# A second round's fourth and fifth attention pair, run as one burst of twelve score tiles

## The chip, the core and the metric

The kernel runs on one core of a Trainium2 chip. The metric is the device time of one execution in microseconds (us), the median of several runs. TensorE (PE, with its weight loads PEld), VectorE (DVE), ScalarE (ACT), GpSimd (POOL) and SyncE (SP) each work through their own list of instructions in order. All transfers between the chip's DRAM and its on-chip memory are issued from SP's list.

## The reference

For 8 batches, 12 heads, 448 positions and a head size of 64, sigmoid attention feeds a gated layer with a product over positions:

```python
scores = scale * np.matmul(q, k.transpose(0, 1, 3, 2)) - np.log(S)
attn = 1.0 / (1.0 + np.exp(-scores))
x = np.matmul(attn, v)                      # then to (batch, seq, 768)
h = np.maximum(x @ w_in, 0.0)               # 768 -> 1024
u, v = h[..., :512], h[..., 512:]
v_n = (v - mean(v)) / np.sqrt(var(v) + 1e-06)
v_s = np.einsum('ts,bsd->btd', w_spatial, v_n) + b_spatial[None, :, None]
out = (u * v_s) @ w_out                     # 512 -> 768
```

All of it is in 32-bit floats. Where one product on TensorE isn't exact enough, the kernel splits an operand into a high and a low part and adds three products.

## The kernel before, in words

**Rounds.** The work runs in four rounds `m` of two batches each. A round has attention (`first_attention` for the first, `attention(m)` for the others), then `v_half` (values through `w_in`), `spatial`, `u_half` and `outputs`. The attention of a round consists of six *pairs* `p` = 0 to 5; a pair is two units (one unit is two heads of one batch), and has six full score tiles (`FIRST` and `SECOND`) and one short one that holds the last 64 keys.

**A pair's work.** For a score tile, TensorE multiplies six times (three products for each of two heads, line 340) into a PSUM tile `psc`, then ACT takes the sigmoid into a tile `at` (line 350). When the tiles of a pair are there, TensorE multiplies them with the values (line 376) into `pav`, and DVE copies `pav` out (`whole`, line 1171). `pair(p)` (line 1185) does six score tiles and then six products. `double(p, extra, early, between, late)` (line 1222) does two pairs as one burst: twelve score tiles, then twelve products. It needs PSUM room, so three of the tiles (`k` = 2, 4, 6) are copied out by DVE first (`move`, lines 1247 and 1249) and the sigmoid is taken later in place (line 1242). It also needs two places more than the ring `free` of tiles has: `extra` names places for the tiles 4 and 6. The hooks `early`, `between` and `late` hold the loads that are issued inside the burst.

**Which rounds do what.** Rounds `m` = 2 and 3 run pair 0, then `double(1)`, then `double(3)` with `extra`. Round `m` = 1, the second, runs `pair(0)`, `double(1)`, `pair(3)`, `pair(4)`. All rounds then do the short tiles (from line 1369) and `pair(5)`.

**Sums that only the second round makes.** During the attention of round 1, POOL forms sums of weights for later rounds, as two generators (`u_sums`, `v_sums`) of which `load_weights(n)` takes the next `n` steps. `v_sums` (line 635) has twelve stages. A stage writes a high and a low part on POOL (a CAST, line 657, and a TENSOR_TENSOR, line 658) into one of four staging tiles, and each fourth stage first makes four differences (line 655) in the tile `v_vals`. A step of the generator issues the store of stage `n` to `tv_dram` on SP (line 664) and then the work of stage `n + 4` on POOL, which overwrites the staging tile that this store reads, so that POOL waits for the store to land. `v_vals` lives in the first half of a large tile, `whole`, that takes turns (tag `shared`) with the output factors of `factors(m)`; its other half is not used.

**What follows on SP.** After the last step of `v_sums`, SP issues four loads of 768 KB (`block_load`, line 1300) into that same large tile, now `factors`, and the first product of `v_half` (line 395, `pv<-factors,x_s`) needs the first of them. The stores, these loads, the loads of the short tiles (`last_loads`, line 1157) and the loads of values (`value_loads`, line 284) all stand in SP's one list. Buffers of values are three (tag `v`), so the load of pair 5's values waits until the last product of pair 3 is done.

**Splits.** `attention_splits` makes the high and low part of a raw tile of queries and keys, in the second round's later pairs on DVE (lines 116 and 117). `following(p)` with the table `groups` says which pairs' splits a pair or burst makes. `last_of_four` names the units whose split stands in the last chunk of `x_s`.

Of the kernel before, what the change touches and what calls it, by code (L numbers as in the profile page):

```python
# [36 lines left out]
def attn_gmlp_kernel(  # L37
# [25 lines left out]
    nc = tc.nc  # L63
    B, NHP, _, _ = qk.shape
    S = out.shape[3]
    D = P // 2
    NCC = out.shape[1]
    DM = NCC * P
    F = w_in.shape[1] // (4 * NCC)
# [27 lines left out]
    mark = small.tile([1, 1], F32, name="mark", bufs=1)  # L97
# [163 lines left out]
    def load_weights(n):  # L261
        for _ in range(n):
            next(weights[0], None)
# [14 lines left out]
    def value_loads(b, hp):  # L278
        vt = work.tile([P, 2 * NFULL + 1, P], F32, tag="v", name=f"v_{b}_{hp}", bufs=3)
        values[b, hp] = vt  # L280
        if b == hp == 0:
            nc.sync.dma_start(vt[:, :NFULL], v[b, hp // 2, :, :NFULL])
        else:
            nc.sync.dma_start(vt, v[b, hp // 2])
# [828 lines left out]
    def attention(m):  # L1113

        first = 2 * NHP * m
        free = []
        last_of_four = (5,) if m == 1 else (5, 9)
        shorts, wholes, lasts, held = {}, {}, {}, {}
        copy = nc.vector.tensor_copy

        def unit(p):
            return units[first + 2 * p]

        def loads(*ns):
            for n in ns:
                attention_loads(*units[first + n])
# [19 lines left out]
        def last_loads(p):  # L1146
            b, hp = unit(p)
            if p in (0, 1, 3, 4):
                raw = work.tile([P, 1024], F32, tag="raw", name=f"last_{b}_{hp}", bufs=4)
                raw = raw.rearrange("p (u c) -> p u c", u=2)  # L1150
            else:
                raw = slot(free, f"last_{b}_{hp}")
                held[p] = free.pop()
            lasts[p] = raw
            for here, there in ((slice(0, HALF), 0), (slice(HALF, HALF + S), HALF + REST)):
                there = slice(there, there + here.stop - here.start)
                nc.sync.dma_start(raw[:, :, here], qk[b, hp : hp + 2, :, there].rearrange("u p c -> p u c"))
# [52 lines left out]
                low_part(n)  # L1210
            return pav

        groups = [(0,), (1, 2), (3,), (4,)] if m == 1 else [(0,), (1, 2), (3, 4)]

        def following(p):
            ends = [g[-1] for g in groups]
# [5 lines left out]
        def double(p, extra, early, between, late=None):  # L1222

            tiles = [(*unit(r), t) for r in (p, p + 1) for t in (*FIRST, *SECOND)]
            ats, tag_of, scores = {}, {}, {}
# [48 lines left out]
                sigmoid(then)  # L1274
            product_of(5)
            sigmoid(6, ats[6])
            nc.scalar.copy(mark, (ats[6][0][:1, :1] if extra else ats[6][:1, 0, :1]))
            product_of(2)
            copy_sums(p, product_of(4), copy)
            between()  # L1280
# [18 lines left out]
        def block_load(k):  # L1299
            nc.sync.dma_start(v_block(m, k).bitcast(F32), w_v_dram[:, k])  # L1300
# [4 lines left out]
        def last_value_loads():  # L1305
            last_v = work.tile([P, 2 * NFULL + 1, P], F32, tag="v", name=f"last_v_{m}", bufs=3)
            last_vs.append(last_v)
            lasts_of = v[2 * m : 2 * m + 2, :, :, NFULL].rearrange("b g p c -> p b g c")
            for i, b, gs in ((0, 0, slice(0, 2)), (2, 0, slice(2, 3)), (3, 1, slice(0, 3))):
                nc.sync.dma_start(last_v[:, i : i + gs.stop - gs.start], lasts_of[:, b, gs])  # L1310

        def after(p):
            for u in ((0, 3), (1, 4, 2, 5))[p - 3]:
                last_loads(u)
            if p == 3:
                value_loads(*unit(5))
            load_weights((3, 8)[p - 3])
            if p == 4:
                for k in range(4):
                    block_load(k)  # L1320

        def second_inside():
            value_loads(*unit(4))
            load_weights(1)

        def inside(p):
            value_loads(*unit(p + 3 - p // 3))
            if p == 3:
                last_loads(2)
            block_load(p)  # L1330

        def early_lasts():
            last_loads(1)
# [2 lines left out]
        extra = []  # L1336
        if m > 1:
            halves_of = [other_tiles(f"oat_{m}", F32)]
            halves_of.append([work.tile([P, 512], F32, tag="wval", name=f"wat_{m}_{i}", bufs=2) for i in range(2)])
            extra = [[t[:, :S] for t in ts] for ts in halves_of]  # L1340
        if m == 1:
            pair(0)
            loads(6, 7)
            value_loads(*unit(3))
            load_weights(1)
            loads(8, 9)
            load_weights(1)
            double(1, [], lambda: None, second_inside)
            loads(10, 11)
            last_value_loads()  # L1350
            load_weights(2)
            for p in (3, 4):
                pair(p)
                after(p)
        else:
            pair(0)
            loads(6, 7)
            value_loads(*unit(3))
            block_load(0)
            loads(8, 9)  # L1360
            double(1, [], lambda: None, lambda: inside(1))
            loads(10, 11)
            last_value_loads()
            block_load(2)
            for u in (0, 3):
                last_loads(u)
            double(3, extra, early_lasts, lambda: inside(3), lambda: last_loads(5))
        last_v, = last_vs
        first_ones, others_of = (0, 3, 1), (4, 2, 5)
        for p in first_ones:  # L1370
# [213 lines left out]
```

## Time and profile before

| what | value |
|---|---|
| median of 3 runs | 633.63 us (632.96 to 634.17) |
| the profiled execution's own time | 632.0 us |
| its span, first to last instruction | 630.2 us |
| PE busy | 625.9 us, 99% |
| DVE busy | 453.7 us, 72% |
| ACT busy | 344.6 us, 55% |
| POOL busy | 106.1 us, 17% |
| DMA | 116.66 MB, mean 185 GB/s |

All times in the rows are counted from the span's start. The profiled execution is 1.6 us below the median of the runs. A "busy" PE is one that has a matmul in its pipe; the share says how little room there is between its matmuls.

### The profile page before, as it was taken

Reading aid. Unit: us, or ns where it says so; the run is one execution under the profiler, and the core shown is the slowest. Engines: PE = TensorE matmul, PEld = TensorE weight load, DVE = VectorE, ACT = ScalarE, POOL = GpSimd, SP = SyncE. Lnnn points to the kernel's source line nnn. Section 1 sums busy time; section 2 is a strip of 40 time slices with the busy share of each in tenths; the row PEclk is TensorE's granted clock in tenths of the full one; section 3 lists DMA queues with packets and bytes.
Section 4 is the critical chain, followed back from the end, with each engine's and each line's share of the span. In section 5 each row is a group of like instructions: output and inputs, shape, how many; then the busy total and the mean of one; then the engine's idle time right before and its main releaser. Section 6 shows DMA issues by size and latency. Waiting matters only on the chain.

```text
span 630.2 us, 10405 instructions
## 1 busy us (share of the span) xinstructions
PE 625.9 (99%) x4029; PEld 492.7 (78%) x4029; DVE 453.7 (72%) x666; ACT 344.6 (55%) x549; POOL 106.1 (17%) x168
## 2 busy tenths in 40 slices
PE   9999999999999999999999999999999999999997
PEld 5555789999765479999975549999997535999997
DVE  6888779998866697356777589635777649845485
ACT  6889385225476776612346696750317667673040
POOL 0000111064968731100000003110000002110000
PEclk9999999999999999999999999999999999999999
DMA  8877731156888876262286924508038681452204
GB/s 315 288 253 221 245 120 33 35 200 255 298 290 289 260 261 231 106 229 99 82 269 233 303 87 161 201 25 327 30 109 319 226 274 51 163 189 56 96 29 147
DMA packets 47746, 116.66 MB, mean 185 GB/s; under 512 B 9040, under 2 KB 26320, under 8 KB 47440
## 3 DMA queue, kind: packets, MB, share of 16 engines
q1 hardware_dynamic: 47696, 115.98, 53.0%
q8 instruction: 32, 0.52, 0.3%
q14 instruction: 18, 0.15, 0.1%
HBM read 91.59 MB, written 24.38 MB: 184 GB/s over the span
## 4 chain that ended last, share of the span: by engine, by line
PE 99%; DVE 1%; issue 0%
PE pav L376 20%; PE pv L395 17%; PE psc L340 14%; PE pw L395 11%; PE pg L395 11%; PE ux L395 7%; PE uy L395 5%; PE pu L395 5%; PE px L395 4%; PE psc L322 3%; DVE whole L1176 0%; PE idle L1481 0%; PE psc L332 0%; PE last L395 0%; DVE cs L1010 0%
## 5 line engine op out<-in xcount | busy, mean ns | idle before, releaser
L350 ACT ACTIVATE at<-psc,bias_s 128x896 f32<-128x896 f32 x105 | 97.7, 1015 | 71.3 <-PE psc L340 53.0
L376 PE MATMUL pav<-at,v 128*64 128x448 f32 (+1 forms) x596 | 113.1, 542 | 0.0
L376 PEld LDWEIGHTS pav<-at,v 128*64 128x64 f32 (+1 forms) x596 | 39.3, 136 | 63.6 <-issue 50.1
L340 PEld LDWEIGHTS psc<-qks 64*128 64x128 f32 x762 | 69.9, 184 | 17.2 <-issue 10.1
L340 PE MATMUL psc<-qks 64*128 64x448 f32 x762 | 82.0, 365 | 0.0
L395 PE MATMUL pg<-w_sp_s,vn 128*128 128x448 f32 x352 | 71.7, 362 | 0.0
L395 PEld LDWEIGHTS pg<-w_sp_s,vn 128*128 128x128 f32 x352 | 65.8, 187 | 4.4
L415 POOL CAST tail<-x_s 128x128 fp32r<-128x128 f32 x40 | 19.3, 515 | 272.4 <-ACT x_s L1179 197.5
L395 PE MATMUL pw<-x_s,factors 128*128 128x448 f32 x261 | 54.0, 362 | 0.0
L1242 ACT ACTIVATE at<-psc,bias_s 128x896 f32<-128x896 f32 x45 | 42.6, 1007 | 18.1 <-PE psc L340 18.1
L395 PEld LDWEIGHTS pw<-x_s,factors 128*128 128x128 f32 x261 | 48.8, 187 | 3.5 <-DVE x_s L893 0.2
L117 DVE TENSOR_TENSOR qks<-raw,qks 128x848 fp32r<-128x848 f32 (+2 forms) x44 | 45.2, 1038 | 5.3 <-ACT qks L116 4.4
L1171 DVE COPY whole<-pav 128x896 f32<-128x896 f32 x15 | 16.4, 1092 | 37.0 <-PE pav L376 36.9
L482 DVE SCALAR_TENSOR_TENSOR vn<-rv,rstd,vn 128x512 fp32r<-128x512 f32 (+1 forms) x26 | 18.8, 748 | 23.5 <-ACT vn L475 23.4
L395 PE MATMUL ux<-x_s,w_u_s 128*128 128x448 f32 x162 | 33.4, 362 | 0.0
L395 PEld LDWEIGHTS ux<-x_s,w_u_s 128*128 128x128 f32 x162 | 30.4, 187 | 2.0
L395 PEld LDWEIGHTS pv<-factors,x_s 128*128 128x128 f32 x243 | 28.0, 188 | 2.1 <-issue 2.1
L395 PE MATMUL pu<-x_s,w_u_s 128*128 128x448 f32 x144 | 29.1, 362 | 0.0
L395 PE MATMUL pv<-factors,x_s 128*128 128x256 f32 x243 | 28.9, 277 | 0.0
L395 PEld LDWEIGHTS pu<-x_s,w_u_s 128*128 128x128 f32 x144 | 27.0, 187 | 1.8
L475 ACT ACTIVATE vn<-rv,rstd 128x512 fp32r<-128x512 f32 (+1 forms) x26 | 17.8, 719 | 18.3 <-POOL rstd L464 18.2
L870 ACT CAST x_s<-g 128x896 fp32r<-128x896 f32 x6 | 5.6, 942 | 38.5 <-DVE g L869 38.5
(225 smaller groups left out, 1123.3 us busy)
## 6 DMA issues: line engine op xcount, KB each, us to landing
raw<-qk_dram SPq DMA_DIRECT2D x46, 456.0 KB, 6.1
v<-v_dram SPq DMA_DIRECT2D x23, 448.0 KB, 5.7
factors<-w_v_dram SPq DMA_DIRECT2D x12, 768.0 KB, 6.2
factors<-t_dram SPq DMA_DIRECT2D x12, 768.0 KB, 4.8
last<-qk_dram SPq DMA_DIRECT2D x18, 448.0 KB, 5.1
factors<-tv_dram SPq DMA_DIRECT2D x9, 768.0 KB, 5.9
factors<-tu_dram SPq DMA_DIRECT2D x9, 768.0 KB, 4.3
wraw<-w_in_dram SPq DMA_DIRECT2D x12, 512.0 KB, 6.0
```

Of the source, the lines that this page charges most:

```text
L117: nc.vector.tensor_sub(lo, src, hi.bitcast(F32))
L322: nc.tensor.matmul(psc[odd * HALF : (odd + 1) * HALF, j, :S], key[rows], query[rows], start=True, stop=True,)
L340: nc.tensor.matmul(psc[:, j, :S], s[rows, a, k : k + P], s[rows, e, REST:PART], start=i == 0, stop=i == len(TERMS) - 1,)
L350: nc.scalar.activation(at, psc[:, :, :S], AF.Sigmoid, bias=bias_s, scale=QK)
L376: nc.tensor.matmul(pav[heads, odd, :S], vt[rows, heads], at[j][rows] if isinstance(at, list) else at[rows, j], start=start, stop=stop)
L395: nc.tensor.matmul(ps, st, mv, start=start and i == 0, stop=i == len(ops) - 1, skip_group_check=not start)
L415: nc.gpsimd.tensor_copy(tails[hp // 2][a][:, :, part], x.bitcast(F32))
L475: nc.scalar.mul(hi, rvs[i][rows], rstd[rows, i : i + 1])
L482: nc.vector.scalar_tensor_tensor(lo, rvs[i][rows], rstd[rows, i : i + 1], hi.bitcast(F32), op0=ALU.mult, op1=ALU.subtract,)
L870: copy(both[:, 0], b)
L1171: copy(whole, pav)
L1242: nc.scalar.activation(a, scores[k] if src is None else a, AF.Sigmoid, bias=bias_s, scale=QK)
```

## The change

`attention(1)` now takes the same way as the other rounds: `pair(0)`, `double(1)`, `double(3)`. The places of the tiles 4 and 6 are two pieces of the unused half of `v_vals`' large tile. Splits of pair 4's second unit stand in the last chunk of `x_s`, as in the other rounds. The steps of the generator and the loads take other places: what stood after `pair(3)` and `pair(4)` now stands ahead of the burst, in its hooks, or behind it.

```diff
-        last_of_four = (5,) if m == 1 else (5, 9)
+        last_of_four = (5, 9)
...
-        groups = [(0,), (1, 2), (3,), (4,)] if m == 1 else [(0,), (1, 2), (3, 4)]
+        groups = [(0,), (1, 2), (3, 4)]
...
-        def after(p):
-            for u in ((0, 3), (1, 4, 2, 5))[p - 3]:
-                last_loads(u)
-            if p == 3:
-                value_loads(*unit(5))
-            load_weights((3, 8)[p - 3])
-            if p == 4:
-                for k in range(4):
-                    block_load(k)
-
-        def second_inside():
-            value_loads(*unit(4))
-            load_weights(1)
-
         def inside(p):
             value_loads(*unit(p + 3 - p // 3))
             if p == 3:
                 last_loads(2)
-            block_load(p)
+            if m == 1:
+                load_weights((1, 3)[p // 2])
+            else:
+                block_load(p)
...
+        else:
+            places = whole[:, NCC * F : NCC * F + 2048].rearrange("p (i j n) -> p i j n", i=2, j=2)
+            extra = [places[:, i, :, :S] for i in range(2)]
+        pair(0)
+        loads(6, 7)
+        value_loads(*unit(3))
         if m == 1:
-            pair(0)
-            loads(6, 7)
-            value_loads(*unit(3))
             load_weights(1)
-            loads(8, 9)
+        else:
+            block_load(0)
+        loads(8, 9)
+        if m == 1:
             load_weights(1)
-            double(1, [], lambda: None, second_inside)
-            loads(10, 11)
-            last_value_loads()
+        double(1, [], lambda: None, lambda: inside(1))
+        loads(10, 11)
+        last_value_loads()
+        if m > 1:
+            block_load(2)
+        for u in (0, 3):
+            last_loads(u)
+        if m == 1:
             load_weights(2)
-            for p in (3, 4):
-                pair(p)
-                after(p)
...
+        double(3, extra, early_lasts, lambda: inside(3), lambda: last_loads(5))
+        if m == 1:
+            load_weights(8)
+            for k in range(4):
+                block_load(k)
```

The first place is PE's list where pair 3 begins. `psc_0_*` and `psc_2_*` are score tiles of pair 3 and pair 4 (the first number is the head unit within the batch, the second the tile), `pav` the products with the values. Before, the six products of pair 3 stand between the two sets of scores:

```order
L340 MATMUL psc_0_5_1984<-qks_1_1872 128x448 x6
L340 MATMUL psc_0_6_1993<-qks_1_1872 128x448 x6
L376 MATMUL pav_0_0_2009<-at_0_0_1955,v_0_1755 64x448 x2
L376 MATMUL pav_0_0_2009<-at_0_1_1964,v_0_1755 64x448 x2
L376 MATMUL pav_0_0_2009<-at_0_2_1973,v_0_1755 64x448 x2
L376 MATMUL pav_0_0_2009<-at_0_4_1982,v_0_1755 64x448 x2
L376 MATMUL pav_0_0_2009<-at_0_5_1991,v_0_1755 64x448 x2
L376 MATMUL pav_0_0_2009<-at_0_6_2000,v_0_1755 64x448 x2
L340 MATMUL psc_2_0_2045<-qks_2_2003 128x448 x6
L340 MATMUL psc_2_1_2054<-qks_2_2003 128x448 x6
```

Now the scores of both pairs stand together, and one of the two tiles in `v_vals` is the last that pair 3's products read:

```order
L340 MATMUL psc_0_6_2003<-qks_1_1872 128x448 x6
L340 MATMUL psc_2_0_2012<-qks_2_1915 128x448 x6
L340 MATMUL psc_2_1_2020<-qks_2_1915 128x448 x6
L340 MATMUL psc_2_2_2029<-qks_2_1915 128x448 x6
L340 MATMUL psc_2_4_2040<-x_s 128x448 x6
L340 MATMUL psc_2_5_2047<-x_s 128x448 x6
L340 MATMUL psc_2_6_2054<-x_s 128x448 x6
L376 MATMUL pav_0_0_2073<-at_0_0_1966,v_0_1755 64x448 x2
L376 MATMUL pav_0_0_2073<-at_0_1_1975,v_0_1755 64x448 x2
L376 MATMUL pav_0_0_2073<-at_0_4_1993,v_0_1755 64x448 x2
L376 MATMUL pav_0_0_2073<-at_0_6_2010,v_0_1755 64x448 x2
L376 MATMUL pav_0_0_2073<-at_0_2_1984,v_0_1755 64x448 x2
```

Pair 3's last product stood after six score tiles and stands after twelve now.

The second place is SP's list from the load of pair 5's values (`v_4`) on. `other_1901`, `other_1902` and `other_87` are staging tiles of `v_sums`: the three stores are those of its stages 2, 3 and 4 (counted from 0). `last_2` and `last_4` are raw tiles of short scores. Before:

```order
L284 DMA v_4_2030<-v_dram 128x896
L664 DMA tv_dram<-other_1901 128x512
L664 DMA tv_dram<-other_1902 128x512
L664 DMA tv_dram<-other_87 128x512
L1157 DMA last_2_2121<-qk_dram 128x2x64
L1157 DMA last_2_2121<-qk_dram 128x2x448
L1157 DMA last_2_2124<-qk_dram 128x2x64
L1157 DMA last_2_2124<-qk_dram 128x2x448
```

Now:

```order
L1157 DMA last_2_2070<-qk_dram 128x2x64
L1157 DMA last_2_2070<-qk_dram 128x2x448
L284 DMA v_4_2096<-v_dram 128x896
L1157 DMA last_4_2098<-qk_dram 128x2x64
L1157 DMA last_4_2098<-qk_dram 128x2x448
L664 DMA tv_dram<-other_1901 128x512
L664 DMA tv_dram<-other_1902 128x512
L664 DMA tv_dram<-other_87 128x512
L1157 DMA last_4_2117<-qk_dram 128x2x64
L1157 DMA last_4_2117<-qk_dram 128x2x448
```

The three stores still stand behind the load of `v_4`, with a short tile's two loads between. POOL's own list is the same in both kernels.

## Rows read from the trace of the kernel before

**Rows 1.** The page, part 4: the chain that ended last, by engine.

```profile
PE 99%; DVE 1%; issue 0%
```

**Rows 2.** Timeline of PE, second round (start, length, line, operation, tiles, count).

```profile
174.38 5.67 PE L340 MATMUL psc<-qks 64*128 64x448 f32 x54
...
190.96 3.87 PE L340 MATMUL psc<-qks 64*128 64x448 f32 x36
...
207.89 2.49 PE L322 MATMUL psc<-last 64*64 64x448 f32 x24
...
225.93 4.26 PE L395 MATMUL pv<-factors,x_s 128*128 128x256 f32 x35
```

**Rows 3.** Timeline of PE, third round, its burst of pairs 3 and 4.

```profile
344.70 5.68 PE L340 MATMUL psc<-qks 64*128 64x448 f32 x54
...
361.29 0.98 PE L322 MATMUL psc<-last 64*64 64x448 f32 x8
```

**Rows 4.** Timeline of SP, second round: issues, in the order of its list.

```profile
199.53 0.34 SPq L284 DMA_DIRECT2D v<-v_dram  x1
199.96 3.54 SPq L664 DMA_DIRECT2D tv_dram<-other  x3
...
208.78 10.23 SPq L664 DMA_DIRECT2D tv_dram<-other  x7
219.07 2.03 SPq L1300 DMA_DIRECT2D factors<-w_v_dram  x4
```

**Rows 5.** Timeline of SP, third round: pair 5's values and what follows.

```profile
356.91 0.34 SPq L284 DMA_DIRECT2D v<-v_dram  x1
357.35 0.89 SPq L1157 DMA_DIRECT2D last<-qk_dram  x2
```

**Rows 6.** Timeline of POOL, second round (in brackets: idle before it, and what ended that).

```profile
192.19 0.81 POOL L657 CAST other<-v_vals 128x256 fp32r<-128x256 f32 x1
193.08 1.42 POOL L658 TENSOR_TENSOR other<-v_vals,other 128x256 fp32r<-128x256 f32 x1
...
205.31 0.39 POOL L657 CAST other<-v_vals 128x256 fp32r<-128x256 f32 x1
205.79 0.73 POOL L658 TENSOR_TENSOR other<-v_vals,other 128x256 fp32r<-128x256 f32 x1
...
207.62 3.16 POOL L655 TENSOR_TENSOR v_vals<-v_vals 128x256 f32<-128x256 f32 x4
...
214.91 0.63 POOL L657 CAST other<-v_vals 128x256 fp32r<-128x256 f32 x1 [2.97 <-DMA tv_dram<-other]
...
218.62 1.78 POOL L415 CAST tail<-x_s 128x128 fp32r<-128x128 f32 x2
```

**Rows 7.** Timeline of DVE, second round.

```profile
192.78 1.12 DVE L117 TENSOR_TENSOR qks<-raw,qks 128x848 fp32r<-128x848 f32 x1
...
218.09 1.52 DVE L1183 TENSOR_TENSOR x_s<-whole,x_s 128x896 fp32r<-128x896 f32 x1
...
220.28 1.09 DVE L1183 TENSOR_TENSOR x_s<-whole,x_s 128x896 fp32r<-128x896 f32 x1
221.29 0.62 DVE L1179 CAST x_s<-whole 128x896 fp32r<-128x896 f32 x1
```

**Rows 8.** DMA issues: count, KB, us to landing; windows of single issues.

```profile
v<-v_dram SPq DMA_DIRECT2D x1, 448.0 KB, 4.2
...
last<-qk_dram SPq DMA_DIRECT2D x1, 448.0 KB, 4.7
...
tv_dram<-other SPq DMA_DIRECT2D x1, 256.0 KB, 6.1
...
factors<-w_v_dram SPq DMA_DIRECT2D x1, 768.0 KB, 5.4
...
factors<-tu_dram SPq DMA_DIRECT2D x1, 768.0 KB, 4.3
```

**Rows 9.** Windows behind the last matmul: engines' busy time, PEclk, DMA share, GB/s.

```profile
626.70:628.50 1.80, 0.00 (x0) 0.00 (x0) 0.35 (x1) 0.00 (x0) 0.00 (x0) 1.00 0.71 254
628.50:630.20 1.70, 0.00 (x0) 0.00 (x0) 0.00 (x0) 0.00 (x0) 0.00 (x0) 0.52 0.02 6
```

More of the change, by code (lines that the diff above doesn't have):

```diff
@@ L1276, in double @@
             sigmoid(6, ats[6])
-            nc.scalar.copy(mark, (ats[6][0][:1, :1] if extra else ats[6][:1, 0, :1]))
+            nc.scalar.copy(mark, (ats[6][0][:1, :1] if isinstance(ats[6], list) else ats[6][:1, 0, :1]))
             product_of(2)
@@ L1340, in attention @@
             extra = [[t[:, :S] for t in ts] for ts in halves_of]
+        else:
[4 more added lines that the diff above has]
+        value_loads(*unit(3))
         if m == 1:
-            pair(0)
-            loads(6, 7)
-            value_loads(*unit(3))
             load_weights(1)
-            loads(8, 9)
+        else:
+            block_load(0)
+        loads(8, 9)
+        if m == 1:
             load_weights(1)
-            double(1, [], lambda: None, second_inside)
-            loads(10, 11)
-            last_value_loads()
-            load_weights(2)
-            for p in (3, 4):
-                pair(p)
-                after(p)
[L1355 to L1367, printed above, removed]
+        double(1, [], lambda: None, lambda: inside(1))
[6 more added lines that the diff above has]
+        if m == 1:
+            load_weights(2)
+        double(3, extra, early_lasts, lambda: inside(3), lambda: last_loads(5))
[3 more added lines that the diff above has]
+                block_load(k)
         last_v, = last_vs
```

## The prediction, made before the change was run

> **What bounds the kernel now.** I read the chain that ended last first: it runs over PE for 99% of the span [rows 1]. So a microsecond counts only where PE gets it or loses it, and whatever other engines do costs nothing until PE waits for it. Then I read PE's timeline through the second round to see what the burst is worth, the same stretch of the third round, which already runs it, as a twin, and last the lists of SP, POOL and DVE beside it, to see which of them PE will wait for when the order of the loads changes. The reader is to see in rows 2 and 3 two lengths of the same work, in rows 4 to 7 a chain SP to POOL to SP that ends at a load which PE needs, and in the row at 225.93 of rows 2 when PE needs it.
>
> **The burst itself.** Pairs 3 and 4 take from 190.96 to 207.89, 16.93 us [rows 2]. In the third round the same 72 + 48 matmuls, as one burst, take from 344.70 to 361.29, 16.59 us [rows 3]; the second round's own burst of pairs 1 and 2 takes 190.96 - 174.38 = 16.58 [rows 2]. So the burst takes 0.34 us off PE's path. The copies by DVE (three more) and the sigmoids in place (two of the tiles in the unused half) lie beside PE in both twins, and I cost them at nothing: if that cover went, PE would show a gap in the burst, and neither twin is longer than 16.59. Splits of pair 4 move ahead of the burst, where the third round makes them too. **Term 1: -0.34 us**, with bounds of 0 (the twins don't carry over) and 0.35.
>
> **What the moved loads do to SP's list.** The stores of the V sums' stages 2, 3 and 4 stand behind the load of pair 5's values. That load waits for the last product of pair 3. Before, it was issued at 199.53 and the first of the three stores at 199.96 [rows 4], because pair 3 was finished after six score tiles and six products. In a burst pair 3's products follow twelve score tiles: the third round's twin issues it at 356.91, 12.21 us after its start [rows 5, 3]. From 190.96 that gives 203.17. Then come two loads of a short tile, 0.89 us of issue [rows 5], so the first store goes out at about 204.5, **4.5 us later than before**. It also queues behind those transfers. In the twin the values took 4.2 us to land and the short tile's second load 4.7 us [rows 8], that is until 362.5, 17.8 us after the burst's start. Here that is 208.7. The twin's short tile (64 and 448 KB) landed 1.4 us behind the values, so I add 0.7 for the store's own 256 KB, and take **209.4** for its landing. Bounds: 208.9 if the loads ahead run half a microsecond faster than the twin's; 210.6 if the store takes 6.1 us, as the slowest did here [rows 8].
>
> **What POOL does with that.** Stage 6 overwrites the staging tile of stage 2, so it can't begin before that landing. Before, it ran at 205.31 without a wait [rows 6]. From stage 6 on POOL has left, in its own rows: stages 6 and 7 from 205.31 to 207.62, 2.3 us; the four differences, 3.2 us; four more stages at the first two's pace, 4.6 us. That is 10.1 us [rows 6]. Before, POOL lost 2.97 us in this stretch waiting for the store of stage 5 at 214.91 [rows 6]; that wait goes, since this store is now out long before POOL comes to it, but it is less than the 4.1 us that appear at stage 6. What is late next is the end of POOL's list: 209.4 + 10.1 = 219.5 instead of 218.62, when nothing disturbs it.
>
> **Something does disturb it.** Where DVE works from on-chip memory to on-chip memory beside POOL, POOL's steps are longer: a CAST took 0.81 against 0.39, a TENSOR_TENSOR 1.42 against 0.73 [rows 6], while DVE ran its splits [rows 7]. So a step waits 0.42 to 0.69 us. Before, POOL's sums ended at 218.62, just as DVE began its run of low and high parts at 218.09, and the two POOL copies that did meet it took 1.78 us together [rows 6, 7]. Now stage 9 ends at 209.4 + 2.3 + 3.2 + 2.3 + 0.7 (one meeting with the low part that DVE makes alone ahead of its run) = 217.9, DVE's run begins at 218.09 - 0.34 = 217.75, and the four steps of stages 10 and 11 all meet it. I take 0.6 us each, nearer the upper row because two of the four stand against L1183, DVE's longest form there: 2.4 us. POOL ends at 217.9 + 2.3 + 2.4 = **222.6**.
>
> The Trainium skill, "SBUF — State Buffer", section "Who interferes with whom", says that a DVE instruction with two inputs there, and a POOL instruction that reads there, share a port, and that the one that issues second stands still until the first is done. The rows agree that POOL stands still, but show less than a whole DVE instruction. With a whole one each (1.09, 0.62, 1.09, 0.62 [rows 7]) the four waits would be 3.4 us and the end 223.6.
>
> **What PE does with that.** SP issues the four loads of 768 KB 0.4 us after POOL's last sum (219.07 against 218.62) [rows 4, 6], so at 223.0. The first of them took 5.4 us [rows 8]; an undisturbed load of that size took 4.3 [rows 8]. I take 5.1, nearer the first because stores stand ahead of it again: 228.1. PE needs it for its first `pv` product, at 225.93 - 0.34 = 225.6 [rows 2]. Before, it landed at 219.07 + 5.4 = 224.5, 1.4 us ahead. **Term 2: PE waits 228.1 - 225.6 = 2.5 us.** The other three blocks follow some 2.1 us apart (768 KB at the pace of 512 KB in 1.4), and each serves 27 products, 3.2 us at 4.26 us for 35 [rows 2], so they add nothing. Lowest: landing at 208.9, no meeting with DVE, 4.3 us for the load: 208.9 + 10.1 + 0.4 + 4.3 = 223.7, no wait at all. Highest: 210.6 + 10.1 + six meetings of 0.69 + 0.4 + 5.4 = 230.6, a wait of 5.0.
>
> **Sum.** -0.34 + 2.5 = +2.2 us. The profiled execution took 632.0, so it would take 634.2; it is 1.6 below the median, and against the median 633.63 the forecast is **635.8**. Behind the wait PE works as before: no stretch there has slack to win it back.
>
> **Rivals.** What a measurement here can tell from no change is about 0.2%, 1.27 us.
>
> *The wait is short.* If the first store lands early, or POOL slips through between DVE's instructions, the first load comes less than 1.6 us late, and the time is 633.3 to 634.9. For it: 1.4 us of slack at 225.93 [rows 2, 4], and a sum whose lowest end shows no wait. Against it: the 4.5 us on SP and POOL's 10.1 us are lists, not chances; only the landings and meetings vary. With no wait at all the burst is left alone, 633.63 - 0.34 = 633.29, faster but by too little to be told from no change.
>
> *More than the burst's gain.* For a time under 632.36 PE would have to win 1.27 us. The twins differ by 0.35 us. Nothing in the rows offers the rest.
>
> *The clock falls in the wait.* After the last matmul at the span's end PE is idle, and the granted clock, 1.00 until 628.50, shows 0.52 from there to the end: 1.2 GHz instead of 2.4, with the last matmul ended by 626.7 [rows 9]. So a wait of 2.5 us may bring it down as well, and the products behind it would run at half speed for a while. No row shows for how long; between nothing and the 3.2 us that the first block's 27 products take at full speed, I take 1.6 more: 637.4. The Trainium skill, "TensorE: Matmul & The Clock Gate", section "Why this matters for your kernels", warns of idle gaps between bursts of matmuls because they throw the clock back to half rate; by that page, too, the gap can cost more than its own length.
>
> *The change doesn't do what it says.* PE's list shows the twelve score tiles together and both tiles in the unused half, so I give that nothing.
>
> **Chances.** Late load, clock kept: 0.45 (635.8, from 634.9 to 638.3). Late load, clock falls: 0.30 (637.4). Short wait or none: 0.22. Over 1.27 us faster: 0.03. Of the short waits nearly all are within 0.2%, so faster 0.03, same 0.22, slower 0.75. The range goes from 633.2, the end without a wait, to 638.3, the highest sum; above lies only a long wait together with a fallen clock.
>
> **What would show it.** Pairs 3 and 4 in about 16.6 us on PE; the load of pair 5's values at 203.2 on SP and the three stores from 204.5; POOL idle before stage 6 until about 209.4, ended by a store's landing; its last CASTs and TENSOR_TENSORs at 0.8 and 1.4 us beside DVE; the four loads at about 223.0; and on PE an idle time of 2 to 3 us before the first `pv`, ended by the load. I am wrong if that first `pv` starts without idling, at about 225.6: then either the stores landed sooner or POOL didn't meet DVE. I am wrong in another way if the burst itself is longer than 16.9 us.

## The result, and the profile after

| what | before | after |
|---|---|---|
| median of 5 runs each | 633.61 us (632.57 to 634.17) | 640.29 us (640.16 to 641.41) |
| ratio, with its 95% interval | | 1.0112 (1.0097 to 1.0127) |
| the profiled execution's own time | 632.0 us | 640.33 us |
| its span | 630.2 us | 638.5 us |
| PE busy | 625.9 us, 99% | 628.9 us, 98% |

The change made the kernel 6.7 us slower. The forecast was 635.8 with a range to 638.3: the direction was right, the time lies outside.

The chain that ended last, on the page of the changed kernel, has left PE for a while [rows 1]:

```profile
PE 94%; POOL 2%; DMA 2%; ACT 1%; issue 0%; SPq 0%; DVE 0%
```

PE's waits (engine, line, what it waited for: us in total, times, longest) name one place:

```profile
PE pv L395 <- DMA factors<-w_v_dram: 5.3, 1, 5.3
```

PE's timeline through the second round (start, length, line, operation, tiles, count; in brackets the idle time ahead and what ended it) answers to [rows 2]:

```profile
175.16 5.69 PE L340 MATMUL psc<-qks 64*128 64x448 f32 x54
...
191.75 5.67 PE L340 MATMUL psc<-qks 64*128 64x448 f32 x54
...
208.33 2.49 PE L322 MATMUL psc<-last 64*64 64x448 f32 x24
...
225.49 0.92 PE L376 MATMUL pav<-at_last,v 128*64 128x448 f32 x4
231.75 8.99 PE L395 MATMUL pv<-factors,x_s 128*128 128x256 f32 x54 [5.34 <-DMA factors<-w_v_dram]
240.58 1.64 PE L395 MATMUL pv<-factors,tail 128*128 128x256 f32 x13
```

At 175.16 this execution is already 0.79 us later than the one of before at the same matmul (174.38). Nothing of the change has run by then, so 0.79 is taken off wherever a time of after is set beside one of before. The burst of pairs 3 and 4 takes 208.33 - 191.75 = 16.58 us in place of 16.93. Then PE waits 5.34 us for the first block, and the 54 products behind it take 240.58 - 231.75 = 8.83 us. In the trace of before the same 54 took 232.17 - 225.93 = 6.24 us:

```profile
225.93 6.41 PE L395 MATMUL pv<-factors,x_s 128*128 128x256 f32 x54
232.17 1.64 PE L395 MATMUL pv<-factors,tail 128*128 128x256 f32 x13
```

The reason is in the windows of the changed kernel (length; busy time and count of PE, PEld, DVE, ACT, POOL; granted clock; DMA share; GB/s):

```profile
226.41:230.49 4.08, 0.00 (x0) 0.00 (x0) 4.04 (x6) 0.56 (x1) 4.08 (x9) 1.00 0.80 240
230.49:231.75 1.26, 0.00 (x0) 0.03 (x1) 0.94 (x2) 0.00 (x0) 1.13 (x2) 0.50 1.04 419
231.75:237.32 5.57, 5.57 (x26) 5.57 (x27) 2.03 (x3) 1.58 (x3) 1.84 (x2) 0.50 1.00 413
237.32:240.60 3.28, 3.28 (x31) 3.28 (x31) 3.21 (x7) 2.52 (x6) 0.00 (x0) 1.00 0.31 121
```

PE's last matmul ended at 226.41. From 230.49 to 237.32 the granted clock is 0.50, 1.2 GHz in place of 2.4, and 5.57 us of that are worked: 26 products where the next 3.28 us hold 31. The account of the change in the profiled pair is therefore -0.35 (burst) + 5.34 (wait) + 2.59 (8.83 - 6.24) = **+7.6 us**. With the 0.79 that stands ahead of it this makes 8.4, and the two profiled executions differ by 8.3. The medians differ by 6.7: the profiled execution of before lies 1.6 below its median, that of after at its own.

What made the block late is a chain over SP, POOL and SP again. Two transfers stand in it, in the chain of the second round (start, length, what); the second ends at 231.62, the first at 211.58:

```profile
205.35 6.22 DMA tv_dram<-other
...
226.81 4.80 DMA factors<-w_v_dram
```

SP's timeline (issues in the order of its list) answers to [rows 4]: the value load at 203.93, two loads of a short tile, and only then the three stores:

```profile
199.39 3.42 SPq L1157 DMA_DIRECT2D last<-qk_dram  x4
203.93 0.34 SPq L284 DMA_DIRECT2D v<-v_dram  x1
204.36 0.90 SPq L1157 DMA_DIRECT2D last<-qk_dram  x2
205.35 1.75 SPq L664 DMA_DIRECT2D tv_dram<-other  x3
...
226.81 2.08 SPq L1300 DMA_DIRECT2D factors<-w_v_dram  x4
```

POOL's timeline answers to [rows 6]. It idles 7.5 us ahead of stage 6, and from 217.87 on nearly every step is long:

```profile
211.63 0.40 POOL L657 CAST other<-v_vals 128x256 fp32r<-128x256 f32 x1 [7.50 <-DMA tv_dram<-other]
...
213.95 3.98 POOL L655 TENSOR_TENSOR v_vals<-v_vals 128x256 f32<-128x256 f32 x4
217.87 0.40 POOL L657 CAST other<-v_vals 128x256 fp32r<-128x256 f32 x1
218.35 1.63 POOL L658 TENSOR_TENSOR other<-v_vals,other 128x256 fp32r<-128x256 f32 x1
219.93 0.80 POOL L657 CAST other<-v_vals 128x256 fp32r<-128x256 f32 x1
220.81 1.46 POOL L658 TENSOR_TENSOR other<-v_vals,other 128x256 fp32r<-128x256 f32 x1
...
225.36 0.99 POOL L658 TENSOR_TENSOR other<-v_vals,other 128x256 fp32r<-128x256 f32 x1
```

DVE's timeline beside it [rows 7]:

```profile
218.29 1.08 DVE L1183 TENSOR_TENSOR x_s<-whole,x_s 128x896 fp32r<-128x896 f32 x1
219.29 1.17 DVE L1179 CAST x_s<-whole 128x896 fp32r<-128x896 f32 x1
220.50 1.17 DVE L1183 TENSOR_TENSOR x_s<-whole,x_s 128x896 fp32r<-128x896 f32 x1
221.59 1.16 DVE L1179 CAST x_s<-whole 128x896 fp32r<-128x896 f32 x1
```

From 217.87 to 226.35 POOL's four stages take 8.48 us. At the 1.15 us that a stage took without company in the trace of before (two from 205.31 to 207.62) they would take 4.6. DVE pays too: its CAST at L1179 takes 1.17 us, against 0.62 alone [rows 7].

### The profile page after: what moved, and what is told of

Its sections match the earlier page's. It is cut to its first block, busy times and chain, and to the rows that moved or that the text cites. A ratio compares the mean times of both kernels' runs of the same rounds, so it can differ in the third digit from the quotient of the medians.

```text
span 638.5 us, 10407 instructions
## 1 busy us (share of the span) xinstructions
PE 628.9 (98%) x4029; PEld 495.5 (78%) x4029; DVE 458.6 (72%) x669; ACT 345.0 (54%) x548; POOL 107.4 (17%) x168
## 4 chain that ended last, share of the span: by engine, by line
PE 94%; POOL 2%; DMA 2%; ACT 1%; issue 0%; SPq 0%; DVE 0%
PE pav L376 17%; PE pv L395 17%; PE psc L340 13%; PE pw L395 11%; PE pg L395 11%; PE ux L395 7%; PE uy L395 5%; PE pu L395 5%; PE px L395 4%; PE psc L322 2%; POOL other L658 1%; DMA tv_dram<-other 1%; DMA factors<-w_v_dram 1%; ACT at L1242 1%; POOL v_vals L655 1%; POOL other L657 1%
## 5 line engine op out<-in xcount | busy, mean ns | idle before, releaser
L350 ACT ACTIVATE at<-psc,bias_s 128x896 f32<-128x896 f32 x93 | 86.8, 1016 | 67.2 <-PE psc L340 45.5
L376 PE MATMUL pav<-at,v 128*64 128x448 f32 (+1 forms) x588 | 111.5, 542 | 0.0
L340 PEld LDWEIGHTS psc<-qks 64*128 64x128 f32 x744 | 68.4, 184 | 16.7 <-issue 10.8
L340 PE MATMUL psc<-qks 64*128 64x448 f32 x744 | 80.3, 366 | 0.0
L1242 ACT ACTIVATE at<-psc,bias_s 128x896 f32<-128x896 f32 x54 | 51.2, 1008 | 23.2 <-PE psc L340 23.2
L395 PE MATMUL pv<-factors,x_s 128*128 128x256 f32 x243 | 31.5, 292 | 5.3 <-DMA factors<-w_v_dram 5.3
L395 PEld LDWEIGHTS pv<-factors,x_s 128*128 128x128 f32 x243 | 30.6, 203 | 7.5 <-issue 7.5
L463 POOL TENSOR_SCALAR rstd<-power 128x1 f32<-128x1 f32 (+1 forms) x19 | 4.5, 237 | 133.4 <-ACT pv L461 98.4
```

The lines of the kernel that those rows point to most:

```text
L340: nc.tensor.matmul(psc[:, j, :S], s[rows, a, k : k + P], s[rows, e, REST:PART], start=i == 0, stop=i == len(TERMS) - 1,)
L350: nc.scalar.activation(at, psc[:, :, :S], AF.Sigmoid, bias=bias_s, scale=QK)
L376: nc.tensor.matmul(pav[heads, odd, :S], vt[rows, heads], at[j][rows] if isinstance(at, list) else at[rows, j], start=start, stop=stop)
L395: nc.tensor.matmul(ps, st, mv, start=start and i == 0, stop=i == len(ops) - 1, skip_group_check=not start)
L1242: nc.scalar.activation(a, scores[k] if src is None else a, AF.Sigmoid, bias=bias_s, scale=QK)
```

## The experiments

Theory 1 was the account above: the block is late because the stores stand behind the value load, and the lost time is the wait plus what the fallen clock takes. Its rivals: the burst itself loses time somewhere; the wait comes from something else that the change moved; the fallen clock is an accident of the profiled run.

### Three stores ahead of the value load

```diff
         def inside(p):
+            if m == 1 and p == 3:
+                load_weights(3)
             value_loads(*unit(p + 3 - p // 3))
...
-                load_weights((1, 3)[p // 2])
+                load_weights((1, 0)[p // 2])
```

> The changed kernel, but the stores of the V sums' stages 2, 3 and 4 stand ahead of the load of pair 5's values on SP instead of behind it. Theory (the stores queue behind a load that waits for pair 3's last product, so POOL is late, so the first 768 KB block is late): store of stage 2 issued at about 202.9 in the after trace's times instead of 205.4, landed by about 207.4 instead of 211.6; POOL's stage 11 done by about 218.4 instead of 226.4; first block landed by about 224, ahead of PE at 226.3, so no idle time before the first pv, clock at full, 633.3 us (between 632.9 and 634.2). Rival A (the block loads are late because their tile is now also read by PE and ACT in the burst): still 5 us of idling, about 640. Rival B (POOL is slow in the burst whatever the stores do, because DVE's copies and splits stand beside it): the first store early, yet POOL's end still at 222 or later, 635 to 638.

Measured: 632.82 us (631.88 to 633.5, 11 runs) against 633.10 for the kernel before on the same chip, a ratio of 0.9991 (0.9982 to 0.9999). PE's timeline of this kernel has no idle time ahead of the first product of `v_half`:

```profile
192.33 5.68 PE L340 MATMUL psc<-qks 64*128 64x448 f32 x54
...
208.91 2.49 PE L322 MATMUL psc<-last 64*64 64x448 f32 x24
...
226.92 6.39 PE L395 MATMUL pv<-factors,x_s 128*128 128x256 f32 x54
```

The burst still takes 16.58 us, and the first block lands at 226.22, 0.7 us before it is needed. Another place for three issues in SP's list thus takes the whole loss away; neither the burst nor the two tiles in the unused half cost anything that shows. Stage 2's store landed at 208.99. The expectation, in the times of the change, was 207.4; this execution began its burst 0.58 us later than that one, so the store was 1.0 us later than expected, and the first block, expected by 224, was too (226.22). Counted from the burst's start the store landed after 16.66 us, where the change has 19.83.

### POOL's last differences made earlier

In the change POOL idles 7.5 us ahead of stage 6, and makes the third group of four differences only behind stage 7. Here they stand right behind stage 5; SP's list is that of the change.

```diff
-            if k == 0:
+            if k == 0 and c < 2:
...
+            if n == 5:
+                w11, w12, w21, w22 = (v_vals[0][:, 4 + r, h * half : (h + 1) * half] for r in range(2) for h in range(2))
+                for a, b, to in ((w12, w11, w11), (w12, w22, w12), (w22, w11, w22), (w21, w22, w21)):
+                    sub(to, a, b)
```

> The changed kernel, its SP list untouched; on POOL the third group of four differences (3.2 us) is made right after stage 5, where POOL idled 7.5 us, instead of after stage 7. Theory (POOL's list behind the late store is on the path, and what of it lies beside DVE's run is longer): stage 6 still starts at about 211.6, but stages 8 to 11 start at 214.0 instead of 217.9 and meet less of DVE, POOL's end at about 219.5 instead of 226.4, first block landed by 225, idle before the first pv 0 to 0.5 us, clock at full, 633.3 to 634.0. Rival A (held tile): about 640. Rival C (only SP's order of issue matters, POOL's length doesn't): about 640.

Measured: 632.56 us (631.63 to 634.43, 10 runs), a ratio of 0.9996 (0.9985 to 1.0006). In POOL's timeline the differences run at 203.50, and stage 6 still begins as late as 211.16:

```profile
203.50 3.15 POOL L662 TENSOR_TENSOR v_vals<-v_vals 128x256 f32<-128x256 f32 x4
211.16 0.40 POOL L657 CAST other<-v_vals 128x256 fp32r<-128x256 f32 x1 [4.50 <-DMA tv_dram<-other]
```

POOL's sums end at 220.15, and PE starts `v_half` without idling at 225.77. So the late store costs only through what POOL has left behind it: 3.2 us less there also take the whole wait away, partly because POOL then comes through before most of DVE's run.

### The late stores put into the kernel before

The kernel before, with pair 3 and pair 4 apart as they were; only the three stores go out later, behind the first two (units 1 and 4) of the four short tiles' loads that follow pair 4.

```diff
             for u in ((0, 3), (1, 4, 2, 5))[p - 3]:
                 last_loads(u)
+                if u == 4:
+                    load_weights(3)
...
-            load_weights((3, 8)[p - 3])
+            load_weights((0, 8)[p - 3])
```

> The kernel before, without burst and without sigmoids in the shared tile; only the stores of stages 2, 3 and 4 are moved on SP, behind the loads of the short tiles of pairs 1 and 4. Theory: the store of stage 2 is issued at about 206.7 instead of 200.0 and lands at about 212.5, stage 6 starts then, POOL's last stages meet DVE's run, first block landed at about 233, PE idle some 7 us before the first pv, the granted clock at half behind it; 641 to 644 us. Rivals A (held tile) and D (the burst itself is what costs): as the kernel before, 633.6.

Measured: 641.47 us in one run. PE's timeline:

```profile
232.02 9.26 PE L395 MATMUL pv<-factors,x_s 128*128 128x256 f32 x54 [4.24 <-DMA factors<-w_v_dram]
```

Without the burst of pairs 3 and 4, late stores alone bring the same picture: POOL waits until 211.97, PE for 4.24 us (less than the 7 expected), and the clock is at half from 231.11 to 237.94. The time lies in the range expected partly by another loss: counted from the start of pairs 1 and 2, PE reached the first product of `v_half` 0.8 us later than in the kernel before (227.78 - 175.40 against 225.93 - 174.38), after a wait at the short tiles, half of whose loads now stand behind the moved stores.

### The wait filled with matmuls

48 products of zeros (96 matmuls in the trace) stand ahead of the first product of `v_half` in the second round; they write a part of PSUM that the real products start afresh. Everything else is the change.

```diff
+        if m == 1:
+            for _ in range(24):
+                for j in range(2):
+                    nc.tensor.matmul(ps[j][:, 1, :128], *(z[j * D : (j + 1) * D] for z in zeros), start=True, stop=True)
```

> The changed kernel with 48 matmuls on zeros (about 5 us) on PE ahead of the first pv product, into a part of PSUM that is written anew later; nothing else is changed. Theory (of the 6.7 us some 2.6 are products at half clock behind the idle time): the wait for the first block stays at about 5.3 us, filled with the zeros' products, the granted clock stays at 1.00 and the 54 products behind take 6.2 us instead of 9.0; 637.0 to 638.2 us. Rival E (the idle time alone makes the loss, the clock's fall costs nothing on the path): 640.3. If the zeros outlast the wait, 638 to 639.

Measured: 639.53 us (638.53 to 639.66, 4 runs), above the range expected. PE's timeline:

```profile
225.88 5.63 PE L705 MATMUL pv<-const-float32-0.0 64*128 64x128 f32 x96
231.61 6.39 PE L395 MATMUL pv<-factors,x_s 128*128 128x256 f32 x54
```

The block lands at 231.57, so the wait is there in full, but the clock stays full and the products take 6.39 us. In the trace they are 2.6 us shorter than in the change (8.99 against 6.39); between the medians, taken in two series of runs, the difference was only 0.8. So it was run again beside the change itself:

> The change as it is, once more, beside the next kernel on one chip, so that the two medians stand against the same runs of the kernel before. Both theories expect 639.8 to 640.8 us, a ratio to before of 1.010 to 1.012, and in the trace an idle time of some 5.3 us on TensorE before the first product of v_half with the granted clock at half for some 7 us from late in the idle time on.

> The change with the same 48 products of zeros (x 128 columns) ahead of the first product of v_half as in the run before. Theory 1 (5.3 us of the loss are the wait for the block, and 2.6 us are its products at half clock): the first block lands as late as in the change, at 231.5, the zeros end just before it, the clock stays full, and the median is 1.5 to 2.6 us under that of the change in the same job. Theory 2 (the clock's share in the profiled run is an accident of that run, and the median loss is the wait alone): within 0.6 us of the change.

Measured, against 632.84 us for the kernel before: the change 641.03 us (640.0 to 642.05, 4 runs), with the wait filled 639.58 us (638.22 to 641.01, 4 runs). The difference is 1.45 us, just under the 1.5 to 2.6 of theory 1 and over the 0.6 of theory 2; but the four runs of each spread over 2.0 and 2.8 us, so these medians alone don't tell the two theories apart. Three things in the profiled runs take from the gain of 2.6. In the second of them the zeros outlasted the wait (the block had landed at 231.98, the products began at 232.44), which loses 0.46 us again, and its 54 products took 6.46 us (232.44 to 238.90) in place of 6.24, at full clock. And both profiled executions with zeros show a wait of PE in the third round that the change doesn't have; the first one's, then the second one's:

```profile
PE pv L395 <- DMA factors<-tv_dram: 0.8, 1, 0.8
PE pv L395 <- DMA factors<-tv_dram: 0.9, 1, 0.9
```

The first of that round's three loads from `tv_dram` took 6.0 and 6.1 us there and 4.4 in the change; why is open. The mean granted clock over the span settles whether the fall is an accident: it was 0.993 to 0.995 in all four runs of the change, and 0.999 to 1.000 in all four with the wait filled and in all seven of before.

### Waits of other lengths

In the kernel with the stores ahead, the order of the four block loads is changed, so that the block PE needs first goes out second or third. In a third kernel only the store of stage 2 goes ahead of the value load.

```diff
-            for k in range(4):
+            for k in (1, 0, 2, 3):
                 block_load(k)
```

The kernel with the block third has `(1, 2, 0, 3)` there; that with one store ahead has the edit of the first experiment with a 1 in place of the 3 and `(1, 2)` in place of `(1, 0)`.

> The kernel with the three stores ahead of the value load, in which the first block landed at 226.22, 0.7 us before TensorE needed it, with one change: the four block loads go out in the order 1, 0, 2, 3. Block 0 should land where block 1 did, at 228.1, so TensorE idles some 1.2 us. Theory 1 (the clock falls only when TensorE has been idle for some time, over 4 us in the change): no fall, the 54 products take 6.4 us, the time is some 1.2 us above that kernel's, 634.0. Theory 2 (any wait of a microsecond for a load brings the clock down): the 54 products take 8 to 9 us, and the time is 636 to 637.

> As the run before, with the order 1, 2, 0, 3. Block 0 should land at 230.0, so TensorE idles some 3.0 us, about what the prediction had forecast for the change. Theory 1 (the clock falls only after a longer idle time than this): no fall, 6.4 us for the 54 products, some 635.8. Theory 2 (a wait of 3 us brings the clock down): the clock falls to half during or just behind the wait, the 54 products take 8 to 9.5 us, 637.5 to 639. Which of the two it is decides whether the prediction's rival on the clock would have come true at the wait that it forecast, or only at the longer one that came.

> Only the store of stage 2 stands ahead of the load of pair 5's values; those of stages 3 and 4 stay behind it. Stage 6 should start at 209 and stage 7 wait until some 212.3, then differences to 216.7, the other stages with some 3 us of meetings to 224, blocks at 224.4, the first landed at 229.3: a wait of some 3 us. If the clock falls behind a wait of 3.6 us and not behind one of 1.6 us, this is a wait of another origin between the two; 635.8 if the clock stays, 637 to 638.5 if it falls. If the store's lateness is not what sets POOL's end, the wait stays at 5 us.

Measured, in one run each: 634.27, 637.14 and 635.67 us (before: 632.84, 632.84 and 633.09). PE's timelines, of the block that goes second:

```profile
227.41 6.60 PE L395 MATMUL pv<-factors,x_s 128*128 128x256 f32 x54 [1.60 <-DMA factors<-w_v_dram]
```

of the one that goes third:

```profile
229.71 7.98 PE L395 MATMUL pv<-factors,x_s 128*128 128x256 f32 x54 [3.61 <-DMA factors<-w_v_dram]
```

and with one store ahead:

```profile
229.77 6.38 PE L395 MATMUL pv<-factors,x_s 128*128 128x256 f32 x54 [2.86 <-DMA factors<-w_v_dram]
```

The two other orders of the blocks were expected to bring waits of 1.2 and 3.0 us and brought 1.60 and 3.61. After 1.60 and 2.86 us the granted clock stays at 1.00 (the 6.60 us with the block second are 0.2 above the 6.41 of before, at full clock all the same). After 3.61 us it doesn't; the windows of that kernel:

```profile
226.10:229.70 3.60, 0.00 (x0) 0.02 (x1) 3.53 (x5) 0.00 (x0) 3.47 (x8) 1.00 1.02 425
229.70:230.00 0.30, 0.29 (x2) 0.30 (x3) 0.02 (x1) 0.00 (x0) 0.17 (x1) 1.00 1.07 451
230.00:233.40 3.40, 3.40 (x18) 3.40 (x17) 0.40 (x1) 1.21 (x2) 0.37 (x1) 0.50 0.76 301
```

The clock goes to half at 230.00, when PE is already at work again, and is back at 233.42. The third kernel is the sharpest run on the prediction: its wait is about the one that was forecast, the clock stays, and its time, 635.67, is 2.6 us above that of before, where -0.34 + 2.86 gives 2.5.

### No second group of differences

The store of stage 2 landed later than the third round's twin had promised. In the change DVE's splits inside the burst were longer than in the twin, since POOL's second group of differences ran beside them, and two short tiles' loads that wait for the splits went out 1.3 us later. This kernel leaves that group out (the second group's four differences aren't formed), so that the splits run alone.

```diff
-            if k == 0:
+            if k == 0 and c != 1:
```

> The change without the second group of four differences on POOL (ahead of stage 4), so the sums of that group aren't formed; everything else stands as in the change. In the change these differences ran from 196.67 to 201.01 beside DVE's splits, which took 1.46, 1.13 and 1.45 us in place of 1.04, 0.59 and 1.04 in the third round's twin, and the loads of the short tiles that wait for them went out 1.3 us later than in the twin. Theory 1 (this is why the store of stage 2 landed 1.4 us later than the prediction took from the twin): the splits take the twin's 1.04, 0.59 and 1.04, the short tile's second load lands 17.8 us after the burst's start, the store 18.5 to 18.6 after it in place of 19.8, POOL meets DVE's run in four to six steps in place of seven, the wait on TensorE is 1.5 to 3 us and the time 634.5 to 636.5. Theory 2 (the store is late for another reason, such as the traffic ahead of it): the splits are short but the store still lands 19.5 us or more behind the burst's start, and the wait stays over 4 us.

Measured: 639.52 us in one run. DVE's timeline shows the splits as short as the twin's:

```profile
196.86 0.59 DVE L116 CAST qks<-raw 128x848 fp32r<-128x848 f32 x1
197.49 1.04 DVE L117 TENSOR_TENSOR qks<-raw,qks 128x848 fp32r<-128x848 f32 x1
198.45 0.59 DVE L116 CAST qks<-raw 128x848 fp32r<-128x848 f32 x1
199.07 1.04 DVE L117 TENSOR_TENSOR qks<-raw,qks 128x848 fp32r<-128x848 f32 x1
```

but POOL's timeline the same late store:

```profile
211.35 0.40 POOL L657 CAST other<-v_vals 128x256 fp32r<-128x256 f32 x1 [8.17 <-DMA tv_dram<-other]
```

The burst began at 191.34 and the store landed at 211.30, 19.96 us later, against 19.83 in the change. The wait is 5.24 us, the clock at half for 6.83 us again. Theory 1 of this run falls: without the longer splits the store lands as late. The value load took 5.6 us here and 5.1 in the change, and 4.2 in the twin [rows 8]. Part of that stood ahead of it. The transfer in front of the value load, a short tile's, landed 2.81 us after the value load's issue in the change (206.74), 2.20 after it here (205.71) and 1.95 in the twin (358.86). From that landing to its own the value load took 2.33 us in the change and 2.30 in the twin, but 3.41 here. So in the change it was late by what was still under way ahead of it; here that had nearly come down in time, and it was late all the same. Why is open.

### Both cures together

The stores ahead and the differences early, in one kernel.

> The change with the three stores ahead of the load of pair 5's values, once more, beside the next kernel. 632.3 to 633.2 us, 0.0 to 0.6 us under the kernel before: no wait ahead of the first product of v_half, clock full, the burst's 0.35 us kept. If the earlier run's gain was chance, it comes out level with before or above.

> The three stores ahead of the load of pair 5's values and the third group of differences made right after stage 5, where POOL idles. If the wait is all that was left to win, each cure alone already takes it away, so both together give the same time as stores_ahead_again within 0.3 us, with the first block landing 2 us or more ahead of TensorE's need instead of 0.7. If the single cures sometimes leave a short wait in the runs that were not profiled, this one comes out 0.3 to 0.8 us faster than stores_ahead_again.

Measured, against 633.09 us for the kernel before: the stores ahead 632.63 us (632.07 to 633.64, 11 runs), both cures 632.49 us (631.62 to 633.01, 11 runs), each with a ratio of 0.9991 (0.9982 to 1.0). The two agree within 0.3 us. The further slack did not come: the first block lands at 227.02 and is needed at 227.16. POOL's timeline of both cures shows the next wait:

```profile
212.51 0.74 POOL L658 TENSOR_TENSOR other<-v_vals,other 128x256 fp32r<-128x256 f32 x1
215.33 1.33 POOL L657 CAST other<-v_vals 128x256 fp32r<-128x256 f32 x1 [2.07 <-DMA tv_dram<-other]
```

That is the store of stage 5, which stands behind the short tiles' loads and which POOL had waited for already in the kernel before [rows 6]. The cured kernels lie a little under the kernel before, by 0.5 and 0.6 us in this series of runs and by 0.3 and 0.5 in the first. The intervals of their ratios end between 0.9999 and 1.0006, so a gain is at the edge of what these runs resolve.

## Why the prediction was right in direction and wrong in size

Four steps failed, and they build on each other: the landing times taken from the twin, the count of POOL's meetings with DVE, both inside the wait (2.5 us forecast, 5.34 measured), then the price of a fallen clock (1.6, measured 2.6), and the sum, which left the fallen clock out and held it apart from a long wait.

**Term 1, the burst: right.** -0.34 us forecast, 16.93 to 16.58 measured, and 16.58 with the stores ahead too.

**SP's list: right.** The value load was forecast for 203.17 and went out at 203.93 - 0.79 = 203.14; the first store for 204.5, and went out at 205.35 - 0.79 = 204.56.

**The store's landing: undersized by 1.4 us.** Forecast 209.4, bounds 208.9 to 210.6; measured 211.58 - 0.79 = 210.8, just outside them. The step that failed is the landing times taken from the twin. The list carried over from the third round, but the landings did not: 5.1 us for the values where the twin's took 4.2, 6.0 for the short tile's second load where it took 4.7, 6.2 for the store. These are the DMA issues of the changed kernel, in windows of single issues (KB, us to landing), in place of [rows 8]; the first row is the value load, then the short tile's and the store's:

```profile
v<-v_dram SPq DMA_DIRECT2D x1, 448.0 KB, 5.1
...
last<-qk_dram SPq DMA_DIRECT2D x1, 448.0 KB, 6.0
...
tv_dram<-other SPq DMA_DIRECT2D x1, 256.0 KB, 6.2
```

A nearer row lay in the same trace. The very load of pair 5's values, in the same round, before the change:

```profile
v<-v_dram SPq DMA_DIRECT2D x1, 448.0 KB, 4.8
```

A stretch's own rows would have been nearer than the twin's. Of the 1.4 us, 0.9 are there when the values land (17.32 us after the burst's start, against 16.46 in the twin), and the tile in front of them was already 0.8 behind the twin. The 0.7 us that the prediction added for the store itself was right (210.81 to 211.58).

**The meetings of POOL and DVE: the price right, the count wrong.** Forecast five meetings, 0.7 + 4 x 0.6 = 3.1 us. Measured, POOL took 226.35 - 211.63 = 14.72 us for what its rows of before give as 10.1, so 4.6: one long difference (0.8) and seven of the eight steps of stages 8 to 11 (3.8 to 3.9, or 0.55 each). Coming 1.4 us later, POOL met DVE's run from stage 8 on, eight meetings in place of five. The error upstream grew here: the landing and the count of meetings belong together, and the bounds had treated them one by one.

The Trainium skill, "SBUF — State Buffer", section "Who interferes with whom", says that the one of the two that issues second stands still until the first is done. The measured steps are shorter than that: in 219.29 to 221.6 the steps take 1.17 and 1.17 us on DVE and 0.80 and 1.46 on POOL, a pair of each in 2.3 us, where the four one after the other would need 0.62 + 1.09 + 0.40 + 0.73 = 2.84. So the four don't all keep each other out for their whole length, and DVE is slowed as well, at its CAST. How the two share the time inside an instruction no run shows.

**Term 2, the wait.** 2.5 forecast, + 1.4 (landing) + 1.5 (meetings: 4.6 - 3.1) - 0.3 (the block's load took 4.8, not 5.1) gives 5.1. The rest is 0.1 us between the block's landing and the first product (231.62 to 231.75) and 0.1 in the issue of the loads. Measured 5.34, above the highest end of 5.0.

**The clock.** The rival "the clock falls in the wait" had 0.30 and is what happened, though not at the wait that it was given for: at 2.86 us, in the one execution that shows it, the clock stayed; it fell in all five profiled executions that waited 3.61 us or longer. Its price was put at 1.6 us and came to 2.6. The windows show what it is made of: what is lost comes close to half of the time that PE works at half clock, 5.57 / 2 = 2.8 against 2.6 measured in the change, and 3.40 / 2 = 1.7 against 1.6 in the kernel with the block third (237.52 - 229.71 = 7.81, less 6.24). The range ended at 638.3 because a long wait together with a fallen clock was held to be unlikely. But the fall came with the longer waits, so these two belonged together. The Trainium skill, "TensorE: Matmul & The Clock Gate", section "Why this matters for your kernels", warns of idle gaps between bursts of matmuls, and the five runs with waits of 3.61 to 5.34 us agree.

**Against the rivals.** The short wait and the gain fell with the trace. That the late stores are the cause is shown from both sides: moving them ahead takes the whole loss away with the burst in place, and moving them back in the kernel before brings a wait of 4.24 us and the fallen clock without the burst of pairs 3 and 4 (in one run, 0.8 us of whose loss has another cause). The late stores cost only together with what POOL has left behind them: 3.2 us less there takes the loss away too, with SP's list as it is in the change.

## What to carry to other kernels

When a burst makes a transfer's issue wait longer, look at what stands behind it in that queue and has nothing to do with it: here three stores, whose place in the list was worth some 7 us, while the burst was worth 0.35. Price a wait on TensorE as two terms that go together, its own length and, where the clock falls with it (here at the five waits of 3.61 us and more, not at 2.86), half of the time worked at half clock afterwards. And take a transfer's time from the stretch itself rather than from a twin elsewhere, with what is still under way ahead of it, since a landing that is late by one microsecond can move a whole list into the company of another engine.

## What the runs showed of the hardware that was not expected

- The granted clock was at 0.50 for 6.83 us in each of the four profiled executions that waited 4.24 to 5.34 us, and for 3.4 us in the one that waited 3.61. In that one it fell when PE had been at work again for 0.3 us.
- Where PE was kept at work through the same wait, with products of zeros, it stayed at full clock: the mean over the span was 0.999 to 1.000 in all eight runs.
- DVE and POOL slow each other to a common pace: 2.3 us for a CAST and a TENSOR_TENSOR on each, with DVE's 0.62 us CAST drawn out to 1.17 and POOL's 0.73 us TENSOR_TENSOR to 1.46.
- The load of pair 5's values in the second round took 4.8, 5.1 and 5.6 us in three kernels (before, the change, no second differences), the same load in the third round 4.2.
- In the kernel with the wait filled the 54 products took 6.46 us in one profiled execution and 6.23 in another, both at a granted clock of 1.00.
